# The first pair's query and key projections by token tile, in a fused attention and MLP kernel

## The chip, the cores and the metric

One core of one Trainium2 chip runs the whole program. The metric is the device time of one execution in microseconds (us), taken over several executions; a profiled execution gives the trace. Engines: PE (TensorE) multiplies matrices, PEld is its loading of stationary operands, DVE is VectorE, ACT is ScalarE, POOL is GpSimd, SP is SyncE, which issues the DMAs here.

## The reference

The input x (2048 tokens of 1024) is layer-normalised. One branch is attention with 32 heads, the other is an MLP on a second normalisation; the result is x + attention times silu(MLP).

```python
xn = _layernorm(x, axis=-1)
s = _A_ref(xn, A_wqkv, A_wo)                 # qkv = xn @ wqkv; softmax(q k^T / sqrt(32)) v; @ wo
g = _silu(_B_ref(xn, B_w1, B_b1, B_w2, B_b2))  # gelu(layernorm(xn) @ w1 + b1) @ w2 + b2
return x + s * g
```

What matters here is only how the attention starts: normalised tokens, 128 at a time (a tile), must be transposed and multiplied with the key, query and value weights before the first scores can be formed.

## The kernel before

A Python program orders all instructions of all engines beforehand; `op` adds an instruction with the keys that it reads and writes, and the waits follow from these (`c` is only the cost that the program's own scheduler assumes). The prologue takes the tokens in pairs of tiles: statistics and normalising on VectorE, with the inverse square root on GpSimd (`norm_pair`; only tile 1's statistics are ScalarE's), transposes on PE with a copy by ScalarE out of PSUM, the memory in banks that PE writes to (`transp`), then keys and queries of the pair (`pair_kq`) and its values (`pair_v`). A bank can be written again only when the copies out of it are done.

```python
def transp(tb):
    ...                                     # cut: tiles from 6 on go by a DMA transpose
    op("tensor", f, r=[("xnb", i), "ident"], w=[("b", bk)], c=("full", 8, 128))   # 8 transposes of 128x128
    op("scalar", lambda e: e.activation(xnT[:, :, tb * 128:(tb + 1) * 128], ..., ACT.Copy),
       r=[("b", bk)], w=[("xnT", tb)], c=903.0)

def pair_kq(p):
    t0, bk = 256 * p, pro_bank()
    for which, nm, dst, off in ((1, "KT", KT, 0), (0, "QT", QT, 256)):
        def f(e, which=which, off=off):
            for dc in range(DC):            # 8 chunks of the contraction
                ins = e.matmul(bank(bk, off, off + 256), lhsT=wq[:, which, dc, 0:128],
                               rhs=xnT[:, dc, t0:t0 + 256], start=dc == 0, stop=dc == DC - 1, ...)
            return ins
        op("tensor", f, r=[("wq", which, s) for s in range(4)] + [("xnT", 2 * p), ("xnT", 2 * p + 1)], ...)
    ...                                     # cut: two copies by ScalarE, to KT and QT

for p in range(3):
    norm_pair(p)
for k, after in ((13, None), (1, 0), (5, 1)):
    op("tensor", lambda e, k=k: warm(e, k), ...)   # k filler products, 128x512
    if after is None:
        transp(0)
    elif after == 0:
        transp(1)
```

After that come, for each pair: `pair_kq`, the transposes of the next pair, `pair_v`, the first scores. The loads are issued in this order: x tiles 0, 1, 2, the K weights, x 3, the Q weights, x 4 and 5, the V weights, the other x tiles.

The softmax here doesn't subtract the row's maximum and nothing guards it: scores larger than these inputs give would overflow.

Of the kernel before, what the change touches and what calls it, by code (L numbers as in the profile page):

```python
# [35 lines left out]
class _Prog:  # L36
# [52 lines left out]
    def op(self, eng, fn, r=(), w=(), dma=None, after=(), c=200.0):  # L89
        deps = list(after)  # L90
        rdy = self.ready(eng, r, w, after)
        same_raw = eng in ("vector", "scalar", "gpsimd")
        for k in r:
            o = self.lastw.get(k)
            if o is not None and (dma or o.dsem or o.eng != eng or same_raw):
                deps.append(o)
        for k in w:
            o = self.lastw.get(k)
            if o is not None and (dma or o.dsem or o.eng != eng or same_raw):
                deps.append(o)  # L100
            for o in self.readers[k].values():
                if dma or o.dsem or o.eng != eng or same_raw:
                    deps.append(o)
        dcount = None
        if dma:
            prev = self.dlast.get(dma)
            if prev is not None:
                deps.append(prev)
            dcount = 16 + (prev.dcount if prev is not None else 0)
        x = _Op(eng, len(self.lists[eng]), fn, deps, dma, dcount)  # L110
        if dma and self.dlast.get(dma) is not None:
            rdy = max(rdy, self.dlast[dma].t)
        self.clock(x, eng, dma, c, rdy)
        if dma:
            self.dlast[dma] = x
        self.lists[eng].append(x)
        self.order.append(x)
        for k in r:
            self.n += 1
            self.readers[k][(eng, self.n) if dma else eng] = x  # L120
        for k in w:
            self.lastw[k] = x
            self.readers[k] = {}
        return x
# [44 lines left out]
def bass_recurrent_scan__mha_block__mixer_channel_mlp__prompt_kernel(  # L169
# [14 lines left out]
    DC = D // 128  # L184
# [23 lines left out]
    with ExitStack() as st:  # L208
        pg = _Prog(nc, st)
        op = pg.op  # L210

        def sb(name, shape, dt):
            return st.enter_context(nc.sbuf_tensor(name, list(shape), dt))
# [4 lines left out]
        ident = sb("ident", [128, 128], BF16)  # L218
        ones = sb("ones", [128, 32], BF16)
        xnT = sb("xnT", [128, DC, S], BF16)  # L220
        OT = sb("OT", [128, HG, S], BF16)
        QT = [sb(f"QT{i}", [128, S], BF16) for i in range(2)]
        KT = [sb(f"KT{i}", [128, S], BF16) for i in range(2)]
# [9 lines left out]
        wq = sb("wq", [128, 3, DC, 256], BF16)  # L233
# [30 lines left out]
        def bank(i, lo=0, hi=512):  # L264
            return ps[:, i * 512 + lo:i * 512 + hi]
# [106 lines left out]
        def pro_bank():  # L372
            pbk["n"] += 1
            return pro_banks[(pbk["n"] - 1) % 3]

        def transp(tb):
            i = tb % NXN
            if tb >= TDMA:
                op("sync", lambda e: e.dma_start_transpose(xnT[:, :, tb * 128:(tb + 1) * 128], xnb[i]),
                   r=[("xnb", i)], w=[("xnT", tb)], dma=f"xt{tb % 4}", c=380)  # L380
                return
            bk = pro_bank()

            def f(e):
                for dc in range(DC):
                    ins = e.transpose(bankb(bk)[:, dc * 128:(dc + 1) * 128], xnb[i][:, dc * 128:(dc + 1) * 128], ident[:])  # L386
                return ins
            op("tensor", f, r=[("xnb", i), "ident"], w=[("b", bk)], c=("full", 8, 128))
            op("scalar", lambda e: e.activation(xnT[:, :, tb * 128:(tb + 1) * 128],
                                                bankb(bk)[:, 0:D].rearrange("p (c t) -> p c t", c=DC), ACT.Copy),  # L390
               r=[("b", bk)], w=[("xnT", tb)], c=903.0)
# [289 lines left out]

        def pair_kq(p):
            t0, bk = 256 * p, pro_bank()
            for which, nm, dst, off in ((1, "KT", KT, 0), (0, "QT", QT, 256)):
                def f(e, which=which, off=off):
                    for dc in range(DC):
                        ins = e.matmul(bank(bk, off, off + 256), lhsT=wq[:, which, dc, 0:128], rhs=xnT[:, dc, t0:t0 + 256],  # L687
                                       start=dc == 0, stop=dc == DC - 1, skip_group_check=True)
                    return ins
                op("tensor", f, r=[("wq", which, s) for s in range(4)] + [("xnT", 2 * p), ("xnT", 2 * p + 1)],  # L690
                   w=[("b", bk, off)] + ([("b", bk)] if off == 0 else []), c=("full", 8, 256))
            for nm, dst, off in (("KT", KT, 0), ("QT", QT, 256)):
                op("scalar", lambda e, dst=dst, off=off: e.activation(dst[0][:, t0:t0 + 256], bank(bk, off, off + 256), ACT.Copy),
                   r=[("b", bk), ("b", bk, 256)], w=[(nm, 0, 2 * p), (nm, 0, 2 * p + 1)], c=263.0)
# [26 lines left out]
        def norm_pair(p):  # L721
            lo, hi = 2 * p, 2 * p + 2
            if p == 0:
                stat(0)
                rstd(0, 1)
                stat_scalar(1)
                xnorm(0)
                bn_half(2, 0)
                xnorm(1)
                bn_half(2, 1)  # L730
                bn_merge(2)
                rstd(2, 3)
                stat(3)
                rstd(3, 4)
                xnorm(2)
                xnorm(3)
            elif p == 1:
                stat(4)
                stat(5)
                rstd(4, 6)  # L740
            else:
                if p < NP - 1:
                    stat(hi)
                for t in (lo, lo + 1):
                    xnorm(t)
                    if t >= TDMA:
                        transp(t)
                if p + 1 < NP:
                    stat(hi + 1)
                    rstd(hi, hi + 2)  # L750
            if p < 2:
                ycoef(p)
# [3 lines left out]
        def warm(e, k):  # L756
            for i in range(k):
                ins = e.matmul(bank(0), lhsT=ident[:], rhs=cold, start=True, stop=True, skip_group_check=True)
            return ins

        for p in range(3):
            norm_pair(p)
        for k, after in ((13, None), (1, 0), (5, 1)):
            op("tensor", lambda e, k=k: warm(e, k), r=["ident"], w=[("b", 0)], c=("full", k, 512))
            if after is None:
                transp(0)
            elif after == 0:
                transp(1)

        def pro_unit(p):  # L770
            if p + 3 < NP:
                norm_pair(p + 3)
            if p >= 2:
                ynorm_pro(p - 2)
            yturn_pro(p - 4)
            if 2 <= p < 2 + 4:
                load_sub(0, p - 2)
            pair_kq(p)
            for t in range(2 * p + 2, 2 * p + 4):
                if t < TDMA:  # L780
                    transp(t)
            pair_v(p)
            if p == 3 + 2:
                turn_bias()
# [33 lines left out]
        for tok in PLAN.split():  # L818
# [8 lines left out]
            for _ in range(num):  # L827
                t = len(flat)
# [120 lines left out]
        while u < NU + LAG or state["qi"] < total or dq or act_tasks or due:  # L949
# [13 lines left out]
            if u >= NP - 1 and state["qi"] < total:  # L963
# [8 lines left out]
                if entry:  # L972
                    it, lo, hi = entry
# [82 lines left out]
```

## Time and profile before

| | kernel before |
|---|---|
| median of 3 runs | 1089.38 us (1088.73 to 1090.94) |
| span of the profiled run | 1086.9 us |
| PE busy | 1077.7 us, 99% |
| ACT busy | 1043.6 us, 96% |
| DVE busy | 627.6 us, 58% |
| first value projection of the prologue starts | 12.68 us |

The table is to be read with care: PE's 99% says nothing about the stretch that the change touches, the first 15 us, which are little more than 1% of the span and in which waiting is what counts. A pair's projections on PE are the lines L687 (keys and queries) and L703 (values).

### The profile page before, as it was taken

Reading aid. Unit: us, or ns where it says so; the run is one execution under the profiler, and the core shown is the slowest. Engines: PE = TensorE matmul, PEld = TensorE weight load, DVE = VectorE, ACT = ScalarE, POOL = GpSimd, SP = SyncE. Lnnn points to the kernel's source line nnn. Section 1 sums busy time; section 2 is a strip of 40 time slices with the busy share of each in tenths; the row PEclk is TensorE's granted clock in tenths of the full one; section 3 lists DMA queues with packets and bytes.
Section 4 is the critical chain, followed back from the end, with each engine's and each line's share of the span. In section 5 each row is a group of like instructions: output and inputs, shape, how many; then the busy total and the mean of one; then the engine's idle time right before and its main releaser. Section 6 shows DMA issues by size and latency. Waiting matters only on the chain.

```text
span 1086.9 us, 61820 instructions
## 1 busy us (share of the span) xinstructions
PE 1077.7 (99%) x29156; PEld 701.4 (65%) x29156; DVE 627.6 (58%) x1396; ACT 1043.6 (96%) x1197; POOL 22.5 (2%) x69
## 2 busy tenths in 40 slices
PE   9999999999999999999999999999999999999998
PEld 6766666666666666666666666666666666666665
DVE  8488843477732576642377743378733387635556
ACT  7899998999999999999999999999999999999993
POOL 4400000000000000000000000000000000000000
PEclk9999999999999999999999999999999999999999
DMA  8944355413474224345233264423264243685444
GB/s 243 178 134 139 116 165 154 126 52 110 118 155 123 67 60 125 104 104 149 90 100 102 70 165 113 125 81 109 81 132 119 91 119 108 194 202 110 108 92 124
DMA packets 209336, 131.92 MB, mean 121 GB/s; under 512 B 52538, under 2 KB 200250, under 8 KB 209082
## 3 DMA queue, kind: packets, MB, share of 16 engines
q1 hardware_dynamic: 209082, 127.97, 43.5%
q8 instruction: 228, 3.74, 1.5%
q14 instruction: 26, 0.21, 0.1%
HBM read 104.87 MB, written 12.06 MB: 108 GB/s over the span
## 4 chain that ended last, share of the span: by engine, by line
PE 57%; ACT 42%; DVE 0%; DMA 0%; issue 0%; POOL 0%; SPq 0%
ACT P L881 38%; PE ps L395 33%; PE ps L869 9%; PE ps L898 6%; PE ps L901 6%; ACT u L565 3%; PE ps L687 1%; PE ps L703 1%; ACT thz L609 0%; DMA OT<-in_A_x_dram 0%; PE ps L386 0%; DVE wq L669 0%; ACT hT L714 0%; DVE zh L605 0%; DVE wq L671 0%
## 5 line engine op out<-in xcount | busy, mean ns | idle before, releaser
L881 ACT ACTIVATE P<-ps 128x1024 bf16<-128x1024 f32 x1024 | 968.1, 1080 | 8.7 <-PE ps L869 3.9
L898 PE MATMUL ps<-P,VP 128*32 128x256 bf16 x4096 | 256.4, 273 | 0.0
L901 PE MATMUL ps<-P,ones 128*32 128x256 bf16 x4096 | 256.3, 273 | 0.0
L395 PE MATMUL ps<-yTc,war 128*32 128x352 bf16 (+1 forms) x5376 | 225.5, 309 | 0.5 <-issue 0.5
L395 PE MATMUL ps<-hT,war 128*32 128x352 bf16 (+1 forms) x5376 | 225.3, 309 | 0.0
L869 PE MATMUL ps<-QT,KT 32*128 32x256 bf16 x4096 | 203.3, 273 | 2.7 <-ACT P L881 0.2
L395 PEld LDWEIGHTS ps<-yTc,war 128*32 128x32 bf16 x5376 | 127.4, 96 | 74.9 <-DVE xb L548 19.2
L395 PEld LDWEIGHTS ps<-hT,war 128*32 128x32 bf16 x5376 | 127.9, 96 | 73.9 <-issue 25.1
L869 PEld LDWEIGHTS ps<-QT,KT 32*128 32x128 bf16 x4096 | 60.7, 92 | 114.4 <-issue 60.4
L605 DVE TENSOR_SCALAR zh<-ps,b2h 128x352 f32<-128x352 f32 (+1 forms) x48 | 27.4, 572 | 182.6 <-PE ps L395 182.6
L548 DVE TENSOR_SCALAR xb<-ps,b1T 128x352 f32<-128x352 f32 (+1 forms) x168 | 96.2, 573 | 48.9 <-PE ps L395 43.9
L571 DVE SCALAR_TENSOR_TENSOR hT<-u,xb 128x352 bf16<-128x352 f32 (+1 forms) x168 | 84.4, 510 | 67.6 <-ACT u L565 67.6
L898 PEld LDWEIGHTS ps<-P,VP 128*32 128x32 bf16 x4096 | 109.3, 97 | 20.4 <-issue 1.3
L901 PEld LDWEIGHTS ps<-P,ones 128*32 128x32 bf16 x4096 | 109.2, 97 | 18.7
L395 PE MATMUL ps<-xnT,wq 128*32 128x352 bf16 (+1 forms) x2688 | 112.7, 309 | 0.0
L395 PEld LDWEIGHTS ps<-xnT,wq 128*32 128x32 bf16 x2688 | 63.7, 96 | 37.2 <-DVE xb L548 9.1
L558 DVE SCALAR_TENSOR_TENSOR u<-u,xb 128x352 f32<-128x352 f32 (+1 forms) x168 | 82.5, 509 | 1.9
L554 DVE TENSOR_TENSOR u<-xb 128x352 f32<-128x352 f32 (+1 forms) x168 | 82.5, 507 | 0.7
L565 ACT ACTIVATE u<-u 128x704 f32<-128x704 f32 (+1 forms) x84 | 71.4, 855 | 0.0
L395 PE MATMUL ps<-xnT,OT 128*32 128x352 bf16 (+2 forms) x1568 | 62.9, 306 | 0.2 <-DVE wq L669 0.2
L395 PE MATMUL ps<-wq,xnT 128*32 128x256 bf16 x1536 | 50.8, 274 | 0.0
L395 PEld LDWEIGHTS ps<-xnT,OT 128*32 128x32 bf16 x1568 | 37.7, 96 | 19.9 <-DVE wq L669 7.7
(61 smaller groups left out, 478.6 us busy)
## 6 DMA issues: line engine op xcount, KB each, us to landing
war<-in_B_w_dram SPq DMA_DIRECT2D x336, 256.0 KB, 3.3
wq<-in_A_wqkv_dram SPq DMA_DIRECT2D x36, 128.0 KB, 2.5
OT<-in_A_x_dram SPq DMA_DIRECT2D x16, 256.0 KB, 5.6
xnT<-in_A_x_dram SPq DMA_DIRECT2D x16, 256.0 KB, 3.2
out_dram<-wq SPq DMA_DIRECT2D x15, 256.0 KB, 2.0
y_scratch<-OT SPq DMA_DIRECT2D x14, 256.0 KB, 2.5
gT_scratch<-gst SPq DMA_DIRECT2D x32, 88.0 KB, 3.2
xnT<-in_A_wo_dram SPq DMA_DIRECT2D x8, 256.0 KB, 4.3
```

Of the source, the lines that this page charges most:

```text
L395: ins = e.matmul(outs(j), lhsT=lhs(j), rhs=rhs, start=start, stop=stop, tile_position=(0, 32 * j), skip_group_check=True)
L548: x0 = op("vector", lambda e: e.tensor_scalar(xb[:, 0:n], bank(bk, 0, n), b1T[:, f:f + 1], None, op0=ALU.add), r=[("b", bk), "b1"], w=[kx] ...
L554: x = op("vector", lambda e: e.tensor_tensor(ub[:, 0:n], xb[:, 0:n], xb[:, 0:n], op=ALU.mult), r=[kx], w=[ku], c=151 + 1.042 * n)
L558: x = op("vector", lambda e: e.scalar_tensor_tensor(ub[:, 0:n], ub[:, 0:n], 1.0 / 0.044715, xb[:, 0:n], op0=ALU.add, op1=ALU.mult), r=[kx, ...
L565: x = op("scalar", lambda e: e.activation(ut[:, :, 0:n], ut[:, :, 0:n], ACT.Tanh, scale=0.7978845608028654 * 0.044715), r=kus, w=kus, c=48 ...
L571: op("vector", lambda e: e.scalar_tensor_tensor(hT[:, fq, 0:n], ut[:, i, 0:n], 1.0, xq[:, 0:n], op0=ALU.add, op1=ALU.mult), r=[kus[i], kq] ...
L605: x0 = op("vector", lambda e: e.tensor_scalar(zh[:, 0:n], bank(bk, 0, n), 0.25, b2h[:, nb:nb + 1], op0=ALU.mult, op1=ALU.add), r=[("b", bk ...
L687: ins = e.matmul(bank(bk, off, off + 256), lhsT=wq[:, which, dc, 0:128], rhs=xnT[:, dc, t0:t0 + 256], start=dc == 0, stop=dc == DC - 1, sk ...
L869: ins = e.matmul(bank(bks[j], kh * 256, (kh + 1) * 256), lhsT=KT[i2][32 * j:32 * j + 32, k0:k0 + 128], rhs=QT[i2][32 * j:32 * j + 32, qb * ...
L881: op("scalar", lambda e, p=p, sl=sl: e.activation(pb[:, 2 * p:2 * p + 2, :, :].rearrange("p a b q -> p (a b q)"), ps[:, sl * 1024:(sl + 1) ...
L898: e.matmul(bankq(ACC, j, 0, QW), lhsT=VP[vp][:, kb, vo + 32 * j:vo + 32 * j + 32], rhs=pb[:, j, kh, :], start=first, stop=False, tile_posi ...
L901: ins = e.matmul(bankq(ACC, j, QW, 2 * QW), lhsT=ones[:, 0:32], rhs=pb[:, j, kh, :], start=False, stop=last, tile_position=(0, 32 * j), sk ...
```

## The change

The intent: tile 0 is transposed and copied about 1.2 us before tile 1. In that time PE only runs fillers. If keys and queries are computed by tile, tile 0's half can go while ScalarE still copies tile 1.

```diff
+            w = 128 if p == 0 else 256
+            for lo in range(0, 256, w):
+                for which, off in ((1, lo), (0, 256 + lo)):
+                    def f(e, which=which, lo=lo, off=off):
+                        for dc in range(DC):
+                            ins = e.matmul(bank(bk, off, off + w), lhsT=wq[:, which, dc, 0:128], rhs=xnT[:, dc, t0 + lo:t0 + lo + w],
+                                           start=dc == 0, stop=dc == DC - 1, skip_group_check=True)
+                        return ins
+                    op("tensor", f, r=[("wq", which, s) for s in range(4)] + [("xnT", t) for t in range((t0 + lo) // 128, (t0 + lo + w) // 128)],
+                       w=[("b", bk), ("b", bk, 256)], c=("full", 8, w))
...
-        for k, after in ((13, None), (1, 0), (5, 1)):
-            op("tensor", lambda e, k=k: warm(e, k), r=["ident"], w=[("b", 0)], c=("full", k, 512))
+        for k, after in ((13, None), (1, 0), (0, 1)):
+            if k:
+                op("tensor", lambda e, k=k: warm(e, k), r=["ident"], w=[("b", 0)], c=("full", k, 512))
```

So the first pair has 32 products of N=128 (N: the columns of the result) in place of 16 of N=256, in the order K0, Q0, K1, Q1, and five fillers are gone.

More of the change, by code (lines that the diff above doesn't have):

```diff
@@ L683, in pair_kq @@
             t0, bk = 256 * p, pro_bank()
-            for which, nm, dst, off in ((1, "KT", KT, 0), (0, "QT", QT, 256)):
-                def f(e, which=which, off=off):
-                    for dc in range(DC):
-                        ins = e.matmul(bank(bk, off, off + 256), lhsT=wq[:, which, dc, 0:128], rhs=xnT[:, dc, t0:t0 + 256],
-                                       start=dc == 0, stop=dc == DC - 1, skip_group_check=True)
-                    return ins
-                op("tensor", f, r=[("wq", which, s) for s in range(4)] + [("xnT", 2 * p), ("xnT", 2 * p + 1)],
-                   w=[("b", bk, off)] + ([("b", bk)] if off == 0 else []), c=("full", 8, 256))
+            w = 128 if p == 0 else 256
[8 more added lines that the diff above has]
+                       w=[("b", bk), ("b", bk, 256)], c=("full", 8, w))
             for nm, dst, off in (("KT", KT, 0), ("QT", QT, 256)):
```

## The prediction

> **What bounds the kernel now.** I read the page first: TensorE (PE) is busy 99% of 1086.9 us and ScalarE (ACT) 96%, and the chain that ended last alternates between them (PE 57%, ACT 42%). The change touches only the prologue, so I went to the chain of waits in order of time, to learn what sets the pace there. Columns: start us, length us, what.
>
> ```profile
> 8.12 0.62 PE ps L386 x8
> 8.74 1.08 PE ps L758 x5
> 9.82 0.04 issue
> 9.86 1.92 PE ps L687 x16
> 11.78 0.89 PE ps L386 x16
> 12.68 1.92 PE ps L703 x16
> 14.60 0.33 PE ps L869 x8
> 14.93 1.85 PE ps L687 x16
> ```
>
> L386 are transposes of normalised tokens, L758 the filler ("warm") products, L687 the query and key projections of a pair of token tiles, L703 its value projection (V), L869 the first scores. From 12.68 us the chain stays on PE without a gap up to 55 us; then ACT's exponentials take over. So whatever this change is worth must appear as an earlier start of L703 at 12.68; all later work shifts by that and by no more. Next, the timeline of that window (start, length, engine, line; the bracket is the idle time and what ended it).
>
> ```profile
> 7.53 1.02 ACT L389 ACTIVATE xnT<-ps 128x1024 bf16<-128x1024 bf16 x1 [0.89 <-PE ps L386]
> 8.58 1.24 PE L758 MATMUL ps<-ident 128*128 128x512 bf16 x5
> 8.78 1.02 ACT L389 ACTIVATE xnT<-ps 128x1024 bf16<-128x1024 bf16 x1 [0.22 <-PE ps L386]
> 9.86 1.92 PE L687 MATMUL ps<-xnT,wq 128*128 128x256 bf16 x16
> 11.39 0.55 DVE L359 TENSOR_SCALAR hT<-OT,mv,lnp 128x1024 bf16<-128x1024 bf16 x1 [0.45 <-POOL lnp L340]
> 11.62 1.06 PE L386 MATMUL ps<-ident,hT 128*128 128x128 bf16 x16
> 12.10 0.38 ACT L693 ACTIVATE QT<-ps 128x256 bf16<-128x256 f32 x1
> 12.68 1.64 PEld L703 LDWEIGHTS ps<-wq,xnT 128*128 128x128 bf16 x16 [0.18 <-DMA wq<-in_A_wqkv_dram]
> ```
>
> The last line carries this prediction: V's weight load stands still for 0.18 us and is released neither by PE nor by ACT, but by the DMA that brings the V weights. I checked it with the view of the weights' tile, restricted to one issue at a time: the V load is issued at 6.67 us and the Q load at 3.30, with
>
> ```profile
> DMA to landing us min/median/max: 6.0/6.0/6.0
> DMA to landing us min/median/max: 6.5/6.5/6.5
> ```
>
> so V lands at 6.67 + 6.0 = 12.67, just when L703 starts, and **Q lands at 3.30 + 6.5 = 9.80**. K, issued at 2.10 with 5.6 to landing, is there at 7.7. The stretches table gives the DMA engines a busy share of 1.06 to 1.13 from 6 to 14 us, 358 to 409 GB/s: the loads are limited by traffic, which the change doesn't touch.
>
> **What the Trainium skill says.** "TensorE: Matmul & The Clock Gate", Back-to-back issue gap, gives N/2.4 + 2.5 ns once warm and N/1.2 cold, and in the same section says that weight loads can raise it, to about 81 ns at N=128. The trace: 16 transposes of N=128 last 1.06 us and one takes 0.219, so the step is (1.06 - 0.219)/15 = 0.056 us; 16 products of N=256 last 1.92, one 0.273, so 0.110. The trace agrees with the formula, and not with 81 ns, at N=128. The same page, Part 1 (the HAM clock gate), has PE at half rate until it has been busy for a window of about 3.4 us, and back to it after an idle window. Here 13 fillers of N=512 start 0.43 us apart from 1.38 to 6.5 us, and at 8.58 five of them step by (1.24 - 0.379)/4 = 0.215: the half rate and the full one. (The granted-clock column says 1.00 all along, so spacing is the thing to look at.) "DMA: Bandwidth & Descriptors", Anatomy of one DMA (it describes the loads that GpSimd issues; these come from SyncE), tells that the semaphore rises only once the last byte is confirmed landed; the wait that ends at 12.68, on the 12.67 landing, agrees.
>
> **The change part by part.** It removes the five fillers after the second transposes, and splits the first pair's 8 key and 8 query products of N=256 into K0, Q0, K1, Q1 of eight products with N=128 each. K0 and Q0 need only tile 0's copy.
>
> 1. Fillers: 5 x 0.215 = 1.08 us of PE, all while PE waits for the second copy to end at 8.78 + 1.02 = 9.80. Taking them away frees no time on the chain by itself.
> 2. K0: tile 0's copy ended at 7.53 + 1.02 = 8.55, K's weights are in at 7.7, and PE leaves the transposes at 8.12 + 8 x 0.056 = 8.57. So K0 runs from about 8.60 to 8.60 + 8 x 0.056 = 9.05.
> 3. Q0: ready by its tokens, but Q's weights land at 9.80. PE is in order, so it stands until about 9.85. **Half of the intended overlap fails here.**
> 4. Q0, K1, Q1 then go together: 24 x 0.056 = 1.34, so PE is free at 9.86 + 1.34 = 11.20, against 9.86 + 16 x 0.110 = 11.62 before. The pair's gain on PE is 0.42 us, not the 0.9 that tile 0's 16 products would have given. The last product ends at 9.86 + 23 x 0.056 + 0.219 = 11.37 against 11.78, so the KT copy on ACT starts at about 11.40 instead of 11.81 and the QT copy ends near 12.07 instead of 12.48.
> 5. Transposes of tiles 2 and 3: tile 2 (normalised at 10.94) goes at 11.20 to 11.65. Tile 3's tokens come from VectorE only at 11.39 + 0.55 = 11.94, a chain without PE in it. So its transposes run from 11.99 to 12.44, against an end at 11.62 + 16 x 0.056 = 12.52 before. Of 0.42 us, **0.08 is left**.
> 6. V: it needs the weights (12.67, as before), PE (12.44 now), and the PSUM bank that the KT and QT copies free (12.07 now, 12.48 before). The latest is the weights. It starts at 12.68 again.
>
> Sum on the path: 0.00 us. If V's weights came early in some run, the old kernel could start V at 12.53 (PE 12.52, the bank 12.48 plus a semaphore), the new at 12.45; so even without the DMA the gain is 0.08 us, 0.007%.
>
> After that nothing else can come from it: the xnT copies of tiles 2 and 3 end about 0.35 us earlier than 14.31, but the next projections, which use them, start at 14.87 because PE is busy. The order of later instructions depends on clocks kept by the kernel's own scheduler, so I worked these by hand from the costs in its code (about order, not about chip time): V begins at 12205 ns in it in both versions, held by its modelled V load (10445 + 1700 + 60), and PE's and ACT's clocks are equal from there on. So the later program should be the same, instruction for instruction. For pairs 1 to 7 the new code emits what the old did; the extra write key adds no wait, because the QT copy reads both keys.
>
> **The rivals.**
> (a) The overlap pays in full: PE 0.9 us earlier through the prologue, 1088.5 us. For it: the chain does run through L687. Against it: Q's landing at 9.80, tile 3's tokens at 11.94 and V's landing at 12.67, three floors one behind the other. Even so it is 0.08%.
> (b) Without fillers the clock falls back. PE's idle time grows: 9.05 to 9.85, 11.65 to 11.99, 12.44 to 12.68, together 1.38 us in 3.6. If it dropped to half rate for one window of 3.4 us, as the page has it, work worth 1.7 us would be added: 1091 us. Against it: no gap exceeds 0.8 us, and a gap of 0.41 us ahead of the 8.12 transposes did not slow the products after it. I give it 6%.
> (c) The landing moves: 22 more PE instructions (11 products net, each with its weight load) alter the instruction fetch, and DMA traffic varies between runs, so V may land some tenths earlier or later; that moves the end by as much, with either sign.
> (d) A new bound on ACT: the copies only come earlier, and ACT waits before V's copy (0.33 us idle) anyway. It changes nothing.
>
> **Range and chances.** 1089.38 - 0.05 (a mean over early and late landings, my estimate) = 1089.3 us. The three runs of before lie between 1088.73 and 1090.94, a spread of 2.2 us that is far larger than any effect above, so the range is that of the runs: 1088.2 to 1090.6, with its lower side leaving room for (a) and its upper for part of (b). Two per cent would be 21.8 us, more than the whole prologue to 14.5 us, so the chances of crossing it either way are about half a per cent each.
>
> **What would show it.** In the changed trace: K0's eight products start near 8.6; PE then idles until about 9.85, released by a DMA on the weights (if by nothing, step 3 is wrong); the group ends and KT's copy starts near 11.4; tile 3's transposes start near 12.0, released by VectorE; L703 starts within 0.15 us of 12.68, released by the V weights' DMA. Products of N=128 stepping by 0.107 instead of 0.056 would show rival (b). L703 starting near 11.9 would make the explanation wrong; another order of later instructions could make the number wrong as well.

## The result, and the profile after

| | before | after |
|---|---|---|
| median of 6 runs | 1089.14 us (1088.53 to 1090.94) | 1089.86 us (1088.91 to 1090.56) |
| ratio, 95% interval | | 1.0003 (0.999 to 1.0016) |
| span of the profiled run | 1086.9 us | 1088.8 us |

Ratios are the mean time of one kernel's runs over that of the other's of the same rounds, so not quite the ratio of the medians. The verdict is "same", that is, within 2%, and the median lies inside the predicted range.

The trace shows more than the time. Here is the timeline of the changed kernel's prologue (start, length, engine, line; the bracket is the idle time and what ended it; the projections are now L689 and L705, the copies to KT and QT L695).

```profile
8.02 0.62 PE L386 MATMUL ps<-ident,hT 128*128 128x128 bf16 x8 [0.53 <-DVE hT L359]
8.48 2.34 PE L689 MATMUL ps<-xnT,wq 128*128 128x128 bf16 x32
9.15 1.49 PEld L689 LDWEIGHTS ps<-xnT,wq 128*128 128x128 bf16 x24 [0.24 <-DMA wq<-in_A_wqkv_dram]
10.86 0.38 ACT L695 ACTIVATE KT<-ps 128x256 bf16<-128x256 f32 x1 [1.16 <-PE ps L689]
11.28 0.55 DVE L359 TENSOR_SCALAR hT<-OT,mv,lnp 128x1024 bf16<-128x1024 bf16 x1 [0.44 <-POOL lnp L340]
11.89 0.62 PE L386 MATMUL ps<-ident,hT 128*128 128x128 bf16 x8 [0.37 <-DVE hT L359]
12.35 1.91 PE L705 MATMUL ps<-wq,xnT 128*128 128x256 bf16 x16
```

The whole group is over at 8.48 + 2.34 = 10.82 instead of 11.78: the change does what it was meant to do, and saves 0.96 us there. (0.10 of this is not its own: tile 1's transposes, which come before anything that it touches, start at 8.02 here and at 8.12 in the trace of the kernel before. So its gain there is 0.86.) But tile 3's transposes still start at 11.89, because VectorE delivers tile 3's tokens at 11.28 + 0.55 = 11.83. And V now starts right behind them, at 12.35, with no wait for a DMA: its weights landed at 11.92 in this run (issued at 6.02, landing 5.9 later).

The chain of waits of the changed kernel, in order of time (start, length, what), shows the second thing:

```profile
11.28 0.55 DVE hT L359
11.83 1.20 DVE stats L324 x2
...
14.66 1.16 DVE stats L324 x2
15.82 0.02 issue
15.84 0.21 DVE mv L328
16.05 0.43 DVE hT L359
16.48 0.05 issue
16.53 1.07 PE ps L386 x16
17.60 1.42 PE ps L705 x13
```

Before, this chain was on PE from 9.86 on. Now it is on VectorE until 16.48: statistics of tiles 4, 5 and 6 one after the other, then the normalising of tile 4, and only then can PE transpose. The weight load of those transposes tells the same in the timeline, after idling although the projections before it were done:

```profile
16.52 0.90 PEld L386 LDWEIGHTS ps<-ident,hT 128*128 128x128 bf16 x16 [0.37 <-DVE hT L359]
```

In the kernel before they began at 16.64, with no idle time. So V's lead of 12.68 - 12.35 = 0.33 us is 0.11 us at 16.6, or, without those 0.10 us, 0.23 and 0.01. By an exponential near 70 us (the 81st record of ScalarE) the changed kernel is 0.22 us ahead, 69.76 against 69.98. It keeps that to 360 us; then it falls behind in two steps of 0.8 to 0.9 us, at 362 and 543 us, and in smaller ones later (and wins 0.38 us back at 419). At the first of them PE paused in the middle of a group of products, and the timeline names nothing that it waited for ("issue"):

```profile
362.49 0.29 PE L901 MATMUL ps<-P,VP 128*32 128x256 bf16 x3 [0.51 <-issue]
```

Since all instructions from the first V on are the same in both programs, this needs a control before anything is read into it.

### The profile page after: what moved, and what is told of

It reads as the page before. It is cut to its first block, busy times and chain, and to the rows that moved or that the text cites. A ratio compares the mean times of both kernels' runs of the same rounds, so it can differ in the third digit from the quotient of the medians.

```text
span 1088.8 us, 61842 instructions
## 1 busy us (share of the span) xinstructions
PE 1078.1 (99%) x29167; PEld 701.4 (64%) x29167; DVE 627.6 (58%) x1396; ACT 1043.9 (96%) x1197; POOL 22.4 (2%) x69
## 4 chain that ended last, share of the span: by engine, by line
PE 57%; ACT 41%; DVE 1%; DMA 0%; issue 0%; POOL 0%; SPq 0%
ACT P L884 37%; PE ps L395 34%; PE ps L872 9%; PE ps L901 6%; PE ps L904 6%; ACT u L565 4%; PE ps L705 1%; PE ps L689 1%; DVE stats L324 0%; DMA OT<-in_A_x_dram 0%; ACT thz L609 0%; DVE wq L669 0%; DVE hT L359 0%; ACT hT L716 0%; DVE wq L671 0%
## 5 line engine op out<-in xcount | busy, mean ns | idle before, releaser
L884 ACT ACTIVATE P<-ps 128x1024 bf16<-128x1024 f32 x1024 | 968.9, 1084 | 10.3 <-PE ps L872 5.4
```

Of the source, the lines that this page charges most:

```text
L884: op("scalar", lambda e, p=p, sl=sl: e.activation(pb[:, 2 * p:2 * p + 2, :, :].rearrange("p a b q -> p (a b q)"), ps[:, sl * 1024:(sl + 1) ...
```

## The experiments

Three theories were to be told apart. **Loads**: the landing of the Q and V weights holds PE, so that no earlier work counts. **VectorE**: the tokens of tiles 3, 4 and 5 hold PE, whatever the weights do. **Clock**: without fillers PE falls back to half rate. For what the end of the run shows there is a fourth matter, the scatter of the 1000 us after the prologue.

All traces start their loads a little differently, so starts are given below, where it says so, **counted from tile 1's transposes** (8.12 us in the kernel before, 8.02 in the changed one); VectorE's chain runs on from there. Each number is a start in the trace minus that of tile 1's transposes, rounded to 0.01. "Landed" is absolute: the V weights' issue plus their time to landing, which the view gives to 0.1 us.

| trace | split | fillers | V landed | V starts | tile 4's transposes | second V | near 70 us |
|---|---|---|---|---|---|---|---|
| before | no | yes | 12.67 | 4.56 | 8.52 | 9.56 | 61.86 |
| before_again | no | yes | 13.34 | 5.27 | 9.21 | 10.27 | 62.57 |
| after | yes | no | 11.92 | 4.33 | 8.51 | 9.42 | 61.74 |
| after_again | yes | no | 12.03 | 4.32 | 8.51 | 9.42 | 61.71 |
| no_fill | no | no | 12.36 | 4.50 | 8.52 | 9.48 | 61.79 |
| split_fill | yes | yes | 12.43 | 4.34 | 8.51 | 9.42 | 61.71 |
| before_halfw | no | yes | 10.23 | 4.49 | 8.52 | 9.47 | 61.94 |
| after_halfw | yes | no | 10.03 | 4.33 | 8.52 | 9.43 | 61.72 |
| before_both | no | yes | 10.23 | 4.49 | 8.42 | 9.47 | 61.77 |
| after_both | yes | no | 10.33 | 3.64 | 7.57 | 8.63 | 60.92 |
| before_stats | no | yes | 13.48 | 5.31 | 9.25 | 10.30 | 62.62 |
| after_stats | yes | no | 13.03 | 4.96 | 8.90 | 9.95 | 62.26 |
| before_late6 | no | yes | 12.30 | 4.50 | 8.42 | 9.48 | 62.81 |
| best | yes | no | 12.62 | 4.68 | 8.60 | 9.66 | 66.49 |

**Control: the kernel before, once more.** No edit.

> The kernel before, unchanged, as a control. If pauses of PE at random places decide the end, its time scatters within 1088.5 to 1091 us, its ratio to itself is 1.000 with an interval of about 0.1%, and its trace agrees with the first one to 0.3 us at the exponentials near 70 us but differs by 0.5 to 2 us at the end. If the changed kernel is truly 0.7 us slower (median 1089.86 against 1089.14), all traces of this one should end 0.5 to 2 us before those of the changed one.

Measured: 1090.17 us median of 5 (1089.14 to 1092.42), ratio to the kernel before 1.0004 (0.9991 to 1.0016): a copy of the kernel is "slower" than the kernel by as much as the changed one was. The span was 1088.4 us against 1086.9 for the same program, and lies between those of the two traces of the changed kernel (1088.3 and 1088.8), so the sign of a truly slower kernel is missing. The expectation of 0.3 us agreement near 70 us was wrong: it is 0.70 us later there (70.68). The chain of waits of this trace says why:

```profile
7.54 5.80 DMA wq<-in_A_wqkv_dram
13.34 0.05 issue
13.38 1.92 PE ps L703 x16
```

The V weights were issued later, at 7.54 instead of 6.67, and PE stood until they landed at 13.34. So the weights are a real floor, and one that moves by more than the change could give.

**The changed kernel, once more.** No edit.

> The changed kernel again. Loads theory (the landing of the Q and V weights holds PE): V starts within 0.1 us of the landing of its weights, be that 12.1 or 12.7. VectorE theory (normalised tokens of tiles 3, 4 and 5 hold PE): tile 3's transposes start near 11.9 and those of tiles 4 and 5 near 16.5, each released by VectorE. Random pauses: the jumps of about 0.8 us near 362 and 543 us of the first trace are not in this one at the same places; if extra instructions cause them, they are. Time 1089 to 1090.5.

Measured: 1090.09 us median of 5, ratio 1.0005 (0.9991 to 1.0018). V's weights landed at 12.03 and V started at 12.69, just behind tile 3's transposes. Tile 3's and tile 4's transposes each follow VectorE, in the timeline (the first row PE, the second its weight load):

```profile
12.23 0.62 PE L386 MATMUL ps<-ident,hT 128*128 128x128 bf16 x8 [0.37 <-DVE hT L359]
16.87 0.91 PEld L386 LDWEIGHTS ps<-ident,hT 128*128 128x128 bf16 x16 [0.37 <-DVE hT L359]
```

This is the VectorE theory's expectation; the loads theory's (V within 0.1 us of its landing) failed here, by 0.66 us. No step of 0.15 us or more against the kernel before appears at 362 or 543 us, where the first trace of the changed kernel lost time (this one has steps of its own, 0.6 us at 321 us and smaller ones later). So the steps don't belong to fixed places of the changed program.

**Only the fillers removed.**

```diff
-        for k, after in ((13, None), (1, 0), (5, 1)):
+        for k, after in ((13, None), (1, 0), (0, 1)):
+            if k: ...
```

> Only the five fillers removed, projections not split. If the fillers only fill a wait, PE starts the first projections at 9.8 to 9.9 as before, V starts within 0.2 us of the kernel before, products keep a step of 0.110 us at N=256. If the clock needs them, the step rises towards 0.21 us and V starts 1 us or more later.

Measured: 1089.82 us (one run). PE idles and then works at its old step:

```profile
9.78 1.92 PE L687 MATMUL ps<-xnT,wq 128*128 128x256 bf16 x16 [1.12 <-ACT xnT L389]
```

16 products take 1.92 us, as with fillers. The clock theory falls for this prologue: an idle 1.12 us at this place costs nothing. Removing the fillers alone neither helps nor harms.

**Only the split, fillers kept.**

```diff
-        for k, after in ((13, None), (1, 0), (0, 1)):
+        for k, after in ((13, None), (1, 0), (5, 1)):
```

(against the changed kernel)

> Only the split, fillers kept. PE is then busy with fillers until about 9.8, so K0 cannot go ahead: 32 products of N=128 at 0.056 end where 16 of N=256 at 0.110 did, near 11.7, and V starts within 0.15 us of the kernel before. If instead the split costs (a step of 0.08 us or more for N=128 with weights reloaded for each), the group ends 0.7 us later.

Measured: 1090.91 us (one run). The 32 products ran from 9.71 to 11.66 (1.95 us), so splitting costs almost nothing. With almost no overlap with tile 1's copy, V starts 4.34 us after tile 1's transposes, the same as in the changed kernel. Counted from tile 1's transposes the group ends at 3.48 here and at 10.82 - 8.02 = 2.80 in the changed kernel. That is the plainest sign that these 0.7 us are lost before V: both versions wait for tile 3's tokens (11.99 in this trace, transposes at 12.05). A small overlap gives the whole 0.16 us at V: the products began 1.53 us after tile 1's transposes, against 1.74 in no_fill.

**Half the early weights, in both versions.** The result is wrong: products read half of the contraction's weights twice, so that K, Q and V need 256 KB each early, not 512.

```diff
-        load_wq(0, (1,))            # and the same for (0,) and (2,)
+        load_wq(0, (1,), 0, 4)      # the other halves after all x tiles
-  lhsT=wq[:, which, dc, 0:128]
+  lhsT=wq[:, which, dc % 4, 0:128]
```

> Wrong result on purpose: the first projections read only half of the contraction's weights (twice over), so that 256 KB instead of 512 KB each of K, Q and V is loaded early; the other halves come after all of x. Projections as in the kernel before, with fillers. Loads theory: V starts as soon as the bank and PE are free, near 12.5. VectorE theory: same start, and the transposes of tiles 4 and 5 still near 16.5.

> The same halved early weights (wrong result on purpose) with the split projections and without fillers. Loads theory: with the weights there, the split pays, V starts 0.4 us or more before that of the same loads without the split, and everything near 70 us is earlier by as much. VectorE theory: tile 3's transposes start at 11.8 to 12.0, V starts at most 0.2 us earlier than without the split, and at the second value projection (near 17.6) and at 70 us the difference is below 0.1 us.

Measured: 1089.6 and 1089.9 us (one run each). The weights are in by 10.3 us, far ahead of need. V starts 4.49 us after tile 1's transposes without the split and 4.33 with it; tile 4's transposes 8.52 in both; the second V 9.47 and 9.43. With the loads floor gone the split gains 0.16 us at the first V, and 0.04 of it is left at the second. The loads theory, as the sole cause, falls. In the timelines, V's weight load without the split, and tile 3's transposes with it:

```profile
12.58 1.66 PEld L704 LDWEIGHTS ps<-wq,xnT 128*128 128x128 bf16 x16
11.91 0.62 PE L387 MATMUL ps<-ident,hT 128*128 128x128 bf16 x8 [0.37 <-DVE hT L360]
```

With the split VectorE holds PE. Without it V has another floor: it writes into the bank that the QT copy on ScalarE frees, and that copy ends at 12.09 + 0.38 = 12.47, 0.11 us before V's weight load. The same 0.11 us lie between them in no_fill, before_late6, before_both and after_both. Near 70 us the difference is 0.22, not below 0.1 as expected: the unsplit trace loses 0.15 us at 51 us, for a reason that was not looked for.

**Half the early weights and a relieved VectorE, in both versions.** In addition, the statistics of tiles 2 to 5 come from half a row (wrong), and tile 6's come after the normalising of tiles 4 and 5.

```diff
-            bn_half(tb, 1)
+            if not 2 <= tb < 6:
+                bn_half(tb, 1)
-                if p < NP - 1:
+                if 2 < p < NP - 1:
                     stat(hi)
                 ...                 # xnorm of the pair's two tiles
+                if p == 2:
+                    stat(hi)
```

> Wrong result on purpose: halved early weights, and also statistics of tiles 2 to 5 from half a row (about 0.6 us of VectorE less for each tile), tile 6's statistics after the normalising of tiles 4 and 5. Projections as before, with fillers. First projections at 9.8 to 11.7, V near 12.4 as PE is the floor; the second pair's transposes follow PE, near 16.4.

> Both floors lowered as in the run beside it, with the split and without fillers. Both theories together: K0, Q0 during the second copy, PE free near 10.7, V at 11.6 to 12.0, and the gain against the same floors without the split, 0.5 to 0.9 us, is still whole at the second value projection and at 70 us. If neither floor matters (the split can't pay for another reason), the difference stays below 0.2 us.

Measured: 1089.23 and 1087.78 us (one run each; with a scatter of 2 us the times can't show 0.85, the traces can). With both floors lowered, V starts 3.64 us after tile 1's transposes with the split, 4.49 without, a gain of 0.85 us; the gain is 0.85 at tile 4's transposes, 0.84 at the second V and 0.85 near 70 us. The chain of waits of the split version now stays on PE, and what it rests on is tile 1's copy on ScalarE:

```profile
8.87 1.03 ACT xnT L392
9.90 0.05 issue
9.95 1.07 PE ps L692 x16
11.01 0.89 PE ps L389 x16
11.91 1.85 PE ps L708 x16
```

PE's 16 products of tile 1 follow the copy (9.95), the transposes follow with no gap, and V 0.1 us behind them, with the QT copy (over at 11.71). This is the change's full worth, and in these runs it exists only here.

**VectorE relieved, the weights whole, in both versions.** The same edit of the statistics alone; wrong as well.

> Wrong result on purpose: only VectorE relieved (statistics of tiles 2 to 5 from half a row, tile 6's after the normalising of tiles 4 and 5), the weights loaded whole. Projections as in the kernel before. PE is the floor: V 4.49 us after tile 1's transposes as with halved weights, or at the landing of its weights if that is later (5.3 in one trace).

> The same relief of VectorE with the split and no fillers. If VectorE alone took the gain, V starts 3.6 to 3.7 us after tile 1's transposes (0.85 earlier than unsplit), and 70 us is reached 0.85 earlier. If the weights are the next floor, V's load waits for their DMA and starts at 12.1 to 12.7, some 4.0 to 4.5 after, so that the gain is 0.0 to 0.5.

Measured: 1089.77 and 1089.37 us (one run each). Both traces had late loads. With the split, Q's weights landed at 10.18 and V's at 13.03; the PE timeline shows both waits:

```profile
8.57 0.61 PE L691 MATMUL ps<-xnT,wq 128*128 128x128 bf16 x8
10.24 1.51 PE L691 MATMUL ps<-xnT,wq 128*128 128x128 bf16 x24 [1.07 <-DMA wq<-in_A_wqkv_dram]
11.59 1.06 PE L388 MATMUL ps<-ident,hT 128*128 128x128 bf16 x16
13.07 1.92 PE L707 MATMUL ps<-wq,xnT 128*128 128x256 bf16 x16 [0.42 <-DMA wq<-in_A_wqkv_dram]
```

This is the picture that the prediction drew for the change (K0 alone, then a wait for Q, then a wait for V), in another run. Relieving VectorE alone was therefore not enough here: V starts at 4.96, not 3.64, and later than the expected 4.0 to 4.5. With weights as early as the earliest seen (11.92 in the changed kernel, 3.90 after tile 1's transposes) it could give about 4.49 - 3.95 = 0.5 us, an estimate from these traces; no run had that. The 0.35 us between the two versions can't be credited to the split, since the two V landings differ by 0.45 us by themselves.

**An attempt at a better version, correct in its result.** Tile 6's statistics are moved behind the normalising of tiles 4 and 5, and V's weights are issued ahead of x tile 5; once without and once with the split.

```diff
-        load_x(5)
         load_wq(0, (2,))
+        load_x(5)
```

(and the move of `stat(hi)` shown above)

> Correct result: tile 6's statistics after the normalising of tiles 4 and 5, V's weights issued ahead of tile 5's load, projections unsplit with fillers. Transposes of tile 4 start 8.4 us after tile 1's (PE's floor, as with both floors lowered), not 8.52; 70 us is reached within 0.1 us of the best traces of the kernel before, and V no longer waits 0.5 us or more for its weights.

> Correct result: the same two moves with the split and no fillers. V 4.33 us after tile 1's transposes (tile 3's tokens still hold it), tile 4's transposes 8.25 to 8.3 after instead of 8.52, 70 us reached 0.2 to 0.3 us earlier than with the split alone. In the total, 0.3 us of 1089 is below the scatter: ratio 0.999 to 1.001, verdict same.

Measured: without the split 1091.67 us (one run), with it 1094.93 us median of 5, ratio 1.0048 (1.0035 to 1.0062). The attempt failed, and of what was expected of `best` only "same" (within 2%) came true, though the loss is clear of noise. The first aim is met in the unsplit trace (tile 4's transposes at 8.42), but it is 0.95 us behind the first trace of the kernel before near 70 us, not within 0.1; with the split Q's weights landed late, at 10.52, and V started at 4.68. V's weights were issued no earlier than elsewhere, at 6.70 and 7.02 us: the load of x tile 4, still ahead of them, alone held SyncE for 2.76 and 2.89 us. The loss comes later. Moving the statistics left VectorE idle for 1.13 us while it waited for GpSimd's result for tiles 4 and 5, which the statistics of tile 6 had covered; tiles 6 and 7 were normalised later, the last of them at 22.25 (20.62 in the changed kernel), and their DMA transposes came too late. Tile 7's was issued at 23.22 and landed at 27.90 (21.58 and 24.43 in the changed kernel): it started 1.6 us later and also took 1.8 us longer, which nothing here explains. In the PE timeline of that run:

```profile
27.95 2.80 PE L689 MATMUL ps<-xnT,wq 128*128 128x256 bf16 x16 [2.79 <-DMA xnT<-hT]
30.54 2.63 PE L705 MATMUL ps<-wq,xnT 128*128 128x256 bf16 x15
```

After an idle 2.79 us the same 16 products took 2.80 us instead of 1.92, and 15 of V's took 2.63, where 16 take 1.92. The stretches of this trace (us, stretch length, busy time and count of PE, PEld, DVE, ACT and POOL, then the granted clock, DMA share and GB/s) show PE's clock:

```profile
24.00:28.00 4.00, 1.22 (x28) 0.51 (x26) 3.93 (x10) 3.55 (x4) 1.15 (x3) 1.00 0.76 137
28.00:32.00 4.00, 4.00 (x23) 2.94 (x24) 3.93 (x9) 0.66 (x2) 1.21 (x3) 0.60 0.65 147
```

The fall did not come in the gap but after it: cut finer, the view gives 1.00 up to 28 us, 0.91 from 28 to 29, 0.50 from 29 to 32 and 0.89 from 32 to 33. So the clock risk that the prediction listed as a rival is real, with a gap of 2.8 us; the gaps that go with the change, up to 1.12 us in no_fill, had no such effect. Whether the load order, the statistics or both cost the time in the other four runs was not separated.

## Why the prediction was right or wrong

The number was right, 1089.3 predicted and 1089.86 measured. That says little for the way there: the predicted range of 2.4 us, as wide as the scatter, would have held the full gain of rival (a) as well (1088.5), and the median came out 0.56 us above the forecast, more than the change's lead in the traces. By the prediction's own signs its reason for V failed: V was to start within 0.15 us of 12.68, released by its weights' DMA, and in neither trace of the changed kernel did that DMA release it.

Of the steps on the way, 1 and 2 held. The fillers covered a wait (no_fill), and K0 ran 0.46 us after tile 1's transposes began, predicted 0.48.

Step 3 (Q lands at 9.80, so half of the overlap fails) was right as a mechanism and wrong in size: Q landed at 9.11, and its load waited 0.24 us; in after_again, with 9.27, it did not show as a wait. In after_stats the wait was 1.07 us. Hence step 4's gain on PE was 0.86 us in the trace, counted from tile 1's transposes, not 0.42.

Step 5 held and is what decided. Tile 3's transposes were predicted at 11.99 with tokens at 11.94; they came at 11.89 with tokens at 11.83, early by the 0.10 us by which that whole trace is. The clean pair (halved weights) shows 0.16 us left at V of the gain ahead of it; predicted was 0.08. For early weights the prediction had V at 12.45 with the split, and that was right (8.12 + 4.33 = 12.45). Without the split it had 12.53, and 8.12 + 4.49 = 12.61 came: its term from the QT copy's end to V was too small, 0.05 us, where V's weight load followed the copy by 0.11.

Step 6 is the step that failed: "The latest is the weights. It starts at 12.68 again." V started at 12.35 and 12.69, behind tile 3's transposes, with its weights in at 11.92 and 12.03. I took one trace's landing for a fixed time. Over the traces with whole weights it ranged from 11.92 to 13.48. That earlier landing is hardly the change's doing: V's load was issued at 6.02 and 6.13 us, ahead of the first changed PE instruction at 8.48, and in after_stats, with the same change, at 7.23. The unevenness is there before: x tile 2, issued at 1.64 us in all ten traces with whole weights, landed between 5.3 and 7.0, and where it came after 6.5 (four traces) V's load was issued at 7.02 to 7.68, elsewhere at 6.02 to 6.70. What delays x tile 2 is open; a different fetch of the instructions, which the prediction named in (c), was not tested.

Also wrong was the claim that from 12.68 on all later work shifts with V. There was a second floor that the chain of waits of the kernel before could not show, because PE was just behind it: tile 4's tokens. In all seven traces with loads in time and VectorE unrelieved in the order of before, tile 4's transposes start 8.51 or 8.52 us after tile 1's, whenever V starts between 4.32 and 4.56. No idle time of PE could point to it. The hint was on VectorE: the statistics of tiles 4 to 6 filled it without a gap, right up to tile 4's normalising. The second V still leads by 0.14 us in the first pair of traces, because in the kernel before it follows the QT copy of the second pair, which ends at 17.21 + 0.42 = 17.63.

Of the rivals, (a), the full gain, is refuted as a result of the change and confirmed as its potential: 0.85 us with both floors lowered, near the 0.9 that it named. (b), the clock, did not occur. (d), no new bound on ScalarE, held for the changed kernel. (c), that the landing moves and the end with it, holds for the landing, while the end is ruled by scatter that comes later: the instructions after the prologue are the same, and from the exponential near 70 us to the last ScalarE instruction the traces of before took 999.90 and 1000.65 us, those of the changed kernel 1001.97 and 1001.18, no_fill 1001.16. That spread of 2 us is ten times the change's lead near 70 us. The split does not lengthen this part by itself: with it after_both took 999.82 us there and after_stats 1000.17. Whether the changed kernel is truly 0.1 us faster can't be read from its time; the traces show it 0.12 to 0.15 us ahead of the best trace of the unchanged kernel near 70 us, counted from tile 1's transposes, and no_fill is within 0.08 of it.

What was not shown: the cause of the pauses in mid-run with no releaser (0.5 to 0.9 us, most at different places in different traces; near 953 to 958 us seven of them lose 0.5 to 1.4 us against after_both, with and without the split).

## What to carry to other kernels

Before working on a wait, find not only what releases it but what would release the next instructions if it were gone: here two other floors, tokens from VectorE and weights from the DMA, stood within a few tenths of a microsecond, and the change paid 0.85 us only with both lowered. When a forecast of "no effect" comes true within the scatter, look at the traces before calling its reason right. A DMA landing read from one trace is a sample; take several traces before calling it the bound, and count from an event that all traces share. An engine's work that looks premature (tile 6's statistics ahead of tile 4's normalising) may be there to cover another engine's latency.

## What the Trainium skill lacked or had wrong

- "TensorE: Matmul & The Clock Gate", Back-to-back issue gap: it gives about 81 ns for each product of N=128 when weights are loaded for every product. Here 16 products of N=128, each with its own weight load, took 1.07 us and one takes 0.219, a step of (1.07 - 0.219)/15 = 0.057 us, the figure that the page gives without weight loads.
- The same page, Part 1: it puts the fall to half rate after an idle window of about 3.4 us. In `best` an idle 2.79 us was enough, and the fall came when PE was already at work again: the products resumed at 27.95 us, the granted clock was 0.91 from 28 to 29 us and 0.50 from 29 to 32, and 16 products took 2.80 us instead of 1.92. An idle 1.12 us changed nothing (1.92).
- No page says what a granted-clock view shows before a trace's first clock record: here it shows 1.00 while the first fillers of N=512 start 0.43 us apart, twice the 0.215 of later ones. The clock gate page warns in general that the clock events of a trace can't be fully trusted; that is not the reason here, since the first record of the kernel before comes at 6.86 us, where the half steps end.
- "DMA: Bandwidth & Descriptors", Anatomy of one DMA: the fit of 2.0 us plus bytes over 436 GB/s (for loads issued by GpSimd) would give an estimated 3.2 us for 512 KB. Under the traffic of this prologue, with loads issued by SyncE, V's 512 KB took 5.6 to 6.0 us from issue to landing, and the landing itself moved by 1.6 us among ten traces of programs that issue it alike, but for the load order in two. No page gives a spread for the landing of one load under such traffic; here nearly all of it was in the issue (6.02 to 7.68 us), while the time from there to landing varied by 0.4.
